# The first 1,160 steps of a fixed instruction order put into another order, in an attention and two-MoE kernel

## The chip, the cores and the metric

The kernel runs on one core of a Trainium2 chip. The metric is the device time of one execution in microseconds (us), lower is better. The engines are TensorE (in the profile PE, its weight loads PEld), VectorE (DVE), ScalarE (ACT), GpSimd (POOL) and SyncE (SP, which here issues nearly all transfers). Each engine takes its instructions strictly in the order in which the program lists them for it, and waits where an operand or a buffer isn't ready.

## The reference, cut to what matters

Inputs: q, k, v of shape (4 batches, 8 heads, 576, 64), phi of (4, 8, 576, 32), and six weight matrices in f32.

```python
a = softmax(phi, axis=2)                       # over the 576 positions
k_m = einsum('bhsm,bhsd->bhmd', a, k)          # 32 memory rows a head
v_m = einsum('bhsm,bhsd->bhmd', a, v)
attn = softmax(scale * q @ k_m.T) @ v_m        # (4, 8, 576, 64)
x = attn.transpose(0, 2, 1, 3).reshape(2304, 512)
x = (x @ w_a) * (x @ w_b) @ w_out              # 512 -> 1536 -> 512
g = x @ w_gate
out = (g / (1 + exp(-g))) * (x @ w_val) @ w2_out
```

## The kernel before, in words

The work is cut into parts, each a Python generator of a few steps; a step emits the instructions of one or two engines. A string, PLAN, lists 2,765 steps by the names of their parts, and one loop emits them in that order:

```python
    for op in PLAN.split():
        if op not in begun:
            begun[op] = work(op)
        next(begun[op], None)
```

So the seventh "p2" in PLAN is the seventh step of part p of batch 2. A dependency from each instruction to the one before it on its engine then fixes the order of all five engines.

The names, with the indices of the batch, the block of features or the tile behind them:

- P, K, L, Q, W: loads, issued by SyncE. P is phi of a batch (576 KB), K and L the first and second two pairs of heads of k and v (1,152 KB each), Q is q (1,152 KB, in two transfers), W a chunk of a weight matrix (512 KB, two words a value, to be decoded). K2, batch 2's qT, Q3 and an accumulator share one place in SBUF, called h7, one after another; phi of batches 0 and 2 and the scores of batch 0 and 2 lie in h9, of 1 and 3 in h10.
- p: the memory of a batch, 14 steps: four maxima on VectorE, one transposition (line 349), a reduction, two small products that spread the maxima (358), addition, exp on ScalarE, the sums k_m and v_m (72 products in the code, 144 matmuls in the profile, line 377, tile kv), the sums of the weights (387), reciprocals, scaling, three transpositions (412, kvT), copies to kb and vt.
- e: four additions over the weights of p. q: transpositions of q (8, 8 or 2 of them, line 437) and the copy of the result to qT, which shares the place h0, h6 or h7. s: the scores of half a batch (40 matmuls, lines 455 and 465, tile sc), maximum, subtraction, exp, denominators, product with them. o: transpositions of the normalised scores (line 502) and their split into a high and a low part, aT.
- c: decoding of a weight chunk, two steps on ScalarE (lines 235 and 237), a clamp, two VectorE operations, one or more on GpSimd. v: v_m times weights (16 matmuls, or 64 from v8 on, line 556), split into vwh and vwl.
- a and b: x @ w_a and x @ w_b of a batch and a block (12 matmuls each, line 541, s1a and s1b); b goes on with the copy, the product of the two and its split into gh and gl. d and f: their product with w_out (12 matmuls, tile s), written to the accumulators acc or added to them by VectorE (line 658).
- x: the first MoE's result is combined and split for the second. E closes the first phase: its pools are released and PSUM is given out anew. U and H are the second phase (lines 789 and 533), A and O load again the decoded weights that were parked in DRAM.

Buffers come from pools. A second table, SLOTS, gives for each kind of buffer the number of the buffer that each request in turn gets; a kind that isn't in the table gets a buffer of the pool of that kind from the builder:

```python
        n = made[key] = made.get(key, -1) + 1
        if key in slots:
            return pool.tile(shape, dt, tag=f"{tag}_{slots[key][n]}", bufs=1, name=name)
        return pool.tile(shape, dt, tag=tag, name=name)
```

In the table b2 are the four PSUM buffers of the first phase (two banks each, taken in turn by p, q, s, o, v, a, b, d and f), and raw the four buffers that weight chunks and A and O are loaded to. SyncE waits, and with it all loads listed behind, where a load's buffer isn't free. A third table, STEPS, says which engine does certain steps; it goes by the number of the part and isn't touched.

Of the kernel before, what the change touches and what calls it, by code (L numbers as in the profile page):

```python
# [18 lines left out]
def kernel(  # L19
# [874 lines left out]
    s2.1 W3.2 W12.1 b1.0 c4.1 c2.2 c9.0 p3 c9.0 s2.0 a1.0 c3.0 s2.1 q3.2 b1.1 s2.0 q3.0 v4 c3.1
    b1.0 q3.1 a1.1 q3.2 s2.0 p3 s2.1 q3.1 p3 q3.0 c3.1 c9.0 b1.0 s2.0 s3.0 c3.0 b1.1 o2.1 o2.1 o2.0
    s3.0 s3.1 o2.1 o2.0 v7 b1.1 v6 s3.0 c2.0 o2.0 a2.1 b2.1 s3.0 s3.1 W12.0 s3.1 v6 b2.0 s3.1 b1.1
    v7 s3.0 b2.1 c2.1 b1.0 v6 s3.0 s3.1 b2.0 s3.1 v7 a2.0 s3.1 W12.2 d1.0.0 W8.0 c3.0 c9.0 s3.0
    b2.0 o3.1 c2.0 o3.0 b2.1 c4.0 c2.1 d1.0.0 o3.0 c2.1 c3.0 d1.2.0 o3.1 c2.1 c2.0 c2.1 c3.2 d1.3.0
    d1.3.0 c3.2 o3.0 o3.1 b3.1 c2.0 b2.1 c4.0 c2.0 a3.1 W5.2 v8 b3.0 b3.1 a3.0 v8 c3.2 d1.2.0 c3.2
    b2.1 c12.0 c4.0 b3.1 d1.1.0 c4.0 b2.0 c3.2 c4.0 b2.0 b3.0 v8 b3.0 v8 b1.2 a1.2 c12.1 c3.2 W5.0  # L900
    c3.2 c12.0 c12.0 d2.0.0 b3.1 c12.1 d1.1.0 b1.2 v8 c12.1 c12.0 d2.1.0 d2.2.0 c12.2 c12.0 c12.0
    b3.0 c12.1 b3.1 a1.3 d2.1.0 c12.1 c12.2 d2.2.0 c12.2 d2.0.0 b0.3 b3.0 b1.2 c12.1 b1.3 d2.3.0
    b0.3 d3.2.0 b1.2 c12.2 d3.0.0 d3.2.0 b1.2 a0.3 c12.2 c12.2 b1.3 d3.1.0 c12.1 d2.3.0 c5.2 d3.3.0
    c5.0 c5.2 c8.0 d3.3.0 b1.3 c12.1 c5.0 b0.3 c5.2 c5.2 b1.3 W8.2 d3.0.0 W8.1 W13.0 c8.0 c5.0 W5.1
    d3.1.0 b0.2 c8.0 b1.3 c5.2 v9 b0.2 a0.2 v9 f0.5.2 c8.0 v9 b0.3 b0.2 c8.0 b0.2 c5.0 b0.3 b3.2 v9
# [17 lines left out]
    c15.2 c15.2 b1.6 v12 b0.6 c16.2 f1.2.4 a1.6 b2.6 c16.2 b2.7 c15.2 b3.7 b2.7 W16.1 W10.2 b0.6
    f1.3.4 c6.2 v12 b3.6 b1.6 c16.0 c9.1 b0.7 a0.7 b1.6 c16.2 b2.7 b0.7 c16.0 c16.2 c16.0 c16.1
    b0.7 c16.1 c9.2 a0.6 c6.2 f1.5.6 c9.2 f1.0.6 f1.4.6 c16.1 c16.1 f1.0.6 f1.3.6 c16.0 b0.7 c16.2
    f1.2.6 f1.1.6 b0.6 v14 b1.7 c9.2 c16.2 f1.5.6 f1.4.6 b1.6 W11.1 c16.1 c16.0 c9.2 c16.1 W17.1
    b0.6 f1.2.6 c16.0 v14 c11.1 b1.7 c16.1 f1.3.6 f1.1.6 c10.2 a1.7 v14 c16.1 b0.8 c10.2 c9.2 b0.7
    v14 b0.6 b1.7 c11.1 b1.7 b1.8 c9.2 W10.1 a1.8 b1.7 a0.8 b1.6 b0.8 c11.1 b1.8 f0.0.6 c10.1 v14
    W10.0 f0.3.6 c10.1 c11.1 f0.2.6 b0.8 c10.2 c11.1 b0.9 f0.3.6 c17.1 f0.0.6 f0.2.6 c17.1 f0.5.6
    c10.0 f0.1.6 c9.2 f0.4.6 c10.1 b1.8 c10.1 b0.9 c10.0 c10.2 c10.2 W11.0 c10.2 f0.1.6 a0.9 v15  # L930
    f0.5.6 b1.8 b1.9 W11.2 f0.4.6 a1.9 b0.8 c17.1 v15 c11.0 b0.9 c10.1 b0.8 c11.0 v15 b2.8 b1.9
    c10.2 W17.2 b1.9 v15 b3.8 v15 b2.9 a3.8 c17.1 W17.0 a2.8 b1.8 c11.0 b1.9 c10.0 b0.9 b3.8 b2.9
    a2.9 b1.9 b2.8 c11.0 c17.0 b2.9 f0.5.8 b0.9 c11.0 f0.3.8 f0.5.8 c10.0 W18.0 b3.8 f0.0.8 b2.8
    c17.0 c17.0 f0.2.8 f0.4.8 f0.1.8 c17.0 c17.1 f0.3.8 c10.0 c17.1 c17.0 c11.2 f0.0.8 v16 b3.8
    b3.9 f0.2.8 a3.9 b2.8 f0.4.8 c17.0 f0.1.8 v16 v16 c17.1 b3.9 b2.8 c11.2 v16 c11.2 b3.8 b2.9
    b0.10 b0.10 v16 A0.12 b2.9 c17.2 c17.1 a0.10 c17.2 c11.2 W18.1 A0.12 b1.11 A0.12 b3.9 c11.2
    b3.9 c11.2 W18.2 f1.0.8 b3.9 b0.11 b1.11 f1.2.8 c18.0 b0.10 c17.2 a0.11 f1.0.8 a1.11 f1.1.8
    b0.11 A0.12 f1.5.8 A0.12 f1.2.8 c17.2 f1.1.8 c18.0 f1.4.8 A0.12 c11.2 f1.5.8 c18.0 f1.3.8 b1.10
    c18.1 b0.10 b0.11 c18.1 A0.12 a1.10 b1.10 b1.11 f1.4.8 b0.11 b1.11 v17 c17.2 c18.1 b0.10 f1.3.8
    b1.10 v17 b0.11 f0.0.10 b1.11 A0.12 f0.1.10 b1.10 c18.2 v17 b1.10 f0.0.10 v17 c18.0 f0.2.10  # L940
# [185 lines left out]
```

## Time and profile before

| | |
|---|---|
| three runs | 835.71 us (median), 831.07 to 835.83 |
| the profiled execution | 836.04 us, of which 834.2 us are the span from the first to the last instruction |
| mean granted clock of TensorE | 0.985 of full speed |
| busy | TensorE 804.0 us (96%), VectorE 573.0 (69%), ScalarE 404.3 (48%), GpSimd 383.1 (46%) |
| instructions | 16,467 |
| transfers | 102.51 MB, 37.1% of the 16 DMA engines' time |

Times in the profile are us from the first instruction of the span. The change of phase (E) is at about 408 us.

### The profile page before, as it was taken

Reading aid. Unit: us, or ns where it says so; the run is one execution under the profiler, and the core shown is the slowest. Engines: PE = TensorE matmul, PEld = TensorE weight load, DVE = VectorE, ACT = ScalarE, POOL = GpSimd, SP = SyncE. Lnnn points to the kernel's source line nnn. Section 1 sums busy time; section 2 is a strip of 40 time slices with the busy share of each in tenths; the row PEclk is TensorE's granted clock in tenths of the full one; section 3 lists DMA queues with packets and bytes.
Section 4 is the critical chain, followed back from the end, with each engine's and each line's share of the span. In section 5 each row is a group of like instructions: output and inputs, shape, how many; then the busy total and the mean of one; then the engine's idle time right before and its main releaser. Section 6 shows DMA issues by size and latency. Waiting matters only on the chain.

```text
span 834.2 us, 16467 instructions
## 1 busy us (share of the span) xinstructions
PE 804.0 (96%) x6540; PEld 752.9 (90%) x6540; DVE 573.0 (69%) x1020; ACT 404.3 (48%) x790; POOL 383.1 (46%) x319
## 2 busy tenths in 40 slices
...
PEclk9789899999999999999999999999999999999999
...
GB/s 326 379 277 118 30 143 142 126 121 159 139 121 89 159 77 80 85 64 1 153 163 193 162 203 147 87 145 121 89 77 108 127 70 50 66 57 128 20 1 113
DMA packets 61772, 102.51 MB, mean 123 GB/s; under 512 B 6400, under 2 KB 35072, under 8 KB 61696
## 3 DMA queue, kind: packets, MB, share of 16 engines
q1 hardware_dynamic: 60896, 100.29, 37.1%
q8 instruction: 51, 0.84, 0.4%
q10 hardware_dynamic: 800, 1.18, 0.4%
q14 instruction: 25, 0.20, 0.1%
...
## 4 chain that ended last, share of the span: by engine, by line
PE 92%; DVE 3%; DMA 1%; ACT 1%; SPq 1%; issue 1%; DVEq 0%
PE p_a L789 18%; PE p_h L533 18%; PE s L533 15%; PE s1b L541 9%; PE p_z L789 9%; PE s1a L541 9%; PE p_c L789 4%; PE s L541 3%; PE vw L556 3%; DMA raw<-in_moe_w_b_dram 1%; PE sc L455 1%; PE kv L377 1%; PE qT L437 1%; PE sc L465 0%; SPq L325 0%
## 5 line engine op out<-in xcount | busy, mean ns | idle before, releaser
L533 PE MATMUL p_h<-o,g 128*128 128x512 f32 x648 | 163.3, 393 | 0.2 <-DVE h_2x L864 0.2
L533 PEld LDWEIGHTS p_h<-o,g 128*128 128x128 f32 x648 | 117.0, 188 | 21.3 <-DVE h_2x L864 0.5
L533 PE MATMUL s<-gh,o 128*128 128x384 f32 x480 | 125.8, 335 | 0.0
L261 POOL TENSOR_TENSOR dec_a<-dec_a,raw 128x512 int32<-128x512 int32 x48 | 66.0, 1375 | 89.1 <-DVE dec_a L249 63.2
L235 ACT ACTIVATE dec_a<-raw 128x512 f32<-128x512 f32 x72 | 48.5, 678 | 82.0 <-POOL w L259 27.1
L533 PEld LDWEIGHTS s<-gh,o 128*128 128x128 f32 x480 | 87.1, 188 | 1.1 <-issue 0.4
L864 DVE TENSOR_TENSOR h_2x<-p_h,h_2x 128x512 f32<-128x512 f32 (+1 forms) x100 | 62.0, 632 | 35.8 <-PE p_h L533 35.5
L533 PE MATMUL s<-gl,o 128*128 128x384 f32 x240 | 80.3, 334 | 0.0
L541 PE MATMUL s1b<-h_1x,vwh 128*128 128x288 f32 x384 | 69.3, 304 | 0.0
L541 PE MATMUL s1a<-h_1x,vwh 128*128 128x288 f32 x384 | 67.2, 297 | 0.3 <-DVE vwl L581 0.3
L541 PEld LDWEIGHTS s1b<-h_1x,vwh 128*128 128x128 f32 x384 | 58.4, 194 | 3.7 <-issue 1.6
L259 POOL TENSOR_TENSOR w<-dec_a,raw 128x512 int32<-128x512 int32 x24 | 31.9, 1331 | 63.8 <-DVE dec_a L249 44.3
L541 PEld LDWEIGHTS s1a<-h_1x,vwh 128*128 128x128 f32 x384 | 56.5, 189 | 2.2 <-issue 1.2
L249 DVE SCALAR_TENSOR_TENSOR dec_a<-raw,dec_a 128x512 int32<-128x512 int32 x72 | 56.0, 778 | 2.5
L174 POOL TENSOR_TENSOR w_u<-again_s,w_u 128x512 fp32r<-128x512 f32 x24 | 32.0, 1333 | 47.7 <-ACT w_u L170 47.0
L174 POOL TENSOR_TENSOR w_g<-again_a,w_g 128x512 fp32r<-128x512 f32 x24 | 31.7, 1320 | 45.7 <-ACT w_g L170 43.0
L840 ACT CAST g<-gate 128x576 fp32r<-128x576 f32 x48 | 32.1, 676 | 38.9 <-PE p_h L533 22.8
L609 DVE TENSOR_TENSOR bs<-s1a,bs 128x576 f32<-128x576 f32 x48 | 35.9, 753 | 21.9 <-PE s1a L541 19.7
L842 DVE TENSOR_TENSOR g<-gate,g 128x576 fp32r<-128x576 f32 x48 | 38.1, 799 | 17.6 <-ACT g L840 17.0
L607 ACT COPY bs<-s1b 128x576 f32<-128x576 f32 x48 | 30.4, 638 | 38.0 <-PE s1b L541 30.3
L237 ACT ACTIVATE raw<-raw 128x512 int32<-128x512 uint32 x72 | 48.4, 679 | 0.0
L807 DVE TENSOR_TENSOR p_c<-p_c,gate 128x288 f32<-128x288 f32 x48 | 22.1, 464 | 37.8 <-PE p_c L789 27.9
...
## 6 DMA issues: line engine op xcount, KB each, us to landing
...
```

The source lines that it names most:

```text
L174: nc.gpsimd.tensor_tensor(out=t[:, :, 1], in0=x, in1=f32(t[:, :, 0]), op=ALU.subtract)
L235: nc.scalar.activation(out=f32(a), in_=f32(hi), func=ACTF.Abs)
L237: nc.scalar.activation(out=lo, in_=lo.bitcast(U32), func=ACTF.Copy, scale=2.0 ** -29)
L249: nc.vector.scalar_tensor_tensor(out=a, in0=hi, scalar=-0x40000000, in1=a, op0=ALU.bitwise_and, op1=ALU.bitwise_or)
L261: nc.gpsimd.tensor_tensor(out=a, in0=a, in1=lo, op=ALU.add)
L533: nc.tensor.matmul(dst, lhsT=l, rhs=r, start=(i == 0), stop=(i == n - 1))
L541: nc.tensor.matmul(p[:, hb, 0:HB], l, x, start=(i == 0), stop=(i == n - 1))
L609: nc.vector.tensor_tensor(out=bs, in0=pa_t.pop((b, f)), in1=bs, op=ALU.mult)
L789: nc.tensor.matmul(bank(where), lhsT=x, rhs=y, start=first and t == 0, stop=t == len(terms) - 1, skip_group_check=True,)
L840: nc.scalar.copy(out=hi, in_=v)
L842: tt(out=lo, in0=v, in1=f32(hi), op=ALU.subtract)
L864: tt(out=dst, in0=src, in1=dst, op=add)
```

## The change

The first 1,160 of PLAN's 2,765 steps stand in another order: the same steps, each part's own steps in their turn. They reach from the start to the first steps of the second phase, a little behind E; the 1,605 steps after them are the same and in the same order. The table SLOTS is emptied, since it numbers requests in the old order, so the builder gives out all these buffers. The words that came with the change: the order was found by a search that counts waits for TensorE's instruction pages; nothing else.

The beginning of the diff, up to the sums of batch 2 (the seventh p2) in both orders, the stretch with the sums of batch 3 in the new order, and the end of the first phase in the new order:

```diff
     SLOTS = """
-    raw
-    0123021230120130231203210230120130230213203212130120231303210323103120120132103210321030321302310213203132321033013021031
-    pm 0101 b2
-    012301201320132031031320123012010231230123013023012301231023013012310321013021321301310213021321032312310320103230313031023132101032013021032031201231202323230132013120321031031232130312031032031312031203010230120303120132031203103201302130
...
     """.split()
...
     PLAN = """
-    P0 K0 W0.1 p0 p0 c0.1 p0 p0 L0 c0.1 W0.0 p0 p0 e0 p0 Q0 P1 c0.1 p0 c0.1 c0.0 W1.1 p0 W1.2 q0.0
-    p0 p0 p0 q0.2 c0.0 q0.0 L1 q0.2 q0.1 p1 K1 p1 c1.1 c0.0 W0.2 p1 p0 c1.1 c1.1 q0.1 c0.1 c0.0 p0
-    c1.1 p1 s0.1 p1 p1 s0.0 c1.1 s0.1 W1.0 s0.1 s0.0 c1.2 s0.1 s0.0 c0.0 v0 s0.0 s0.1 e1 Q1 c1.2 v0
-    s0.1 c0.2 c0.2 P2 p1 c1.0 L2 s0.0 W2.2 s0.0 s0.1 p1 c1.0 p1 v0 s0.0 c1.0 c1.0 p1 c1.2 K2 o0.1
-    o0.0 c1.0 P3 o0.1 q1.2 q1.0 Q2 W4.1 p1 o0.0 o0.1 p1 v1 q1.2 o0.0 p2 v1 b0.0 p1 v1 c1.2 c1.2 p2
-    c0.2 p2 b0.1 q1.0 p1 b0.0 a0.1 b0.1 c0.2 p2 c1.2 v3 c2.2 p2 a0.0 c0.2 W3.0 q1.1 b0.1 v2 c2.2
-    b0.0 c2.2 b0.1 c0.2 v3 p2 v2 c1.2 b0.0 b0.1 c0.2 s1.0 v3 p2 q1.1 p3 v2 e2 s1.1 c4.1 c4.1 s1.0
...
+    P0 L0 W0.1 W0.0 c0.1 c0.0 c0.0 p0 p0 K0 p0 c0.1 c0.1 p0 p0 p0 W1.1 c0.0 c0.1 Q0 p0 e0 P1 W1.2
+    p0 c1.1 c0.0 q0.0 p0 c1.1 p0 q0.0 q0.2 K1 p0 p0 q0.1 L1 p1 c1.1 p1 q0.2 p1 p0 p1 c1.1 p0 s0.0
+    W1.0 c0.1 c0.0 q0.1 p1 c1.2 p1 s0.1 s0.0 s0.0 v0 s0.0 s0.1 s0.1 v0 s0.0 s0.0 Q1 p1 v0 c1.1 e1
+    p1 W0.2 s0.0 s0.1 s0.1 P2 c1.0 c1.0 s0.1 s0.1 c1.0 c1.2 o0.1 L2 p1 q1.2 c1.0 p1 o0.1 p1 o0.0
+    o0.0 c0.2 q1.0 o0.1 c1.0 v1 W2.2 p1 q1.2 o0.0 c0.2 v1 p2 p1 b0.0 c1.2 p2 P3 v1 c0.2 b0.1 W4.1
+    c0.2 q1.0 a0.1 p1 b0.0 c0.2 p2 c1.2 p2 a0.0 b0.1 Q2 K2 q1.1 p2 s1.0 c2.2 c0.2 p2 c0.2 b0.0 c1.2
+    p3 q1.1 b0.0 c1.2 s1.0 s1.1 v2 L3 c2.2 b0.1 v3 v2 v3 s1.0 s1.1 q2.0 s1.0 v2 e2 v3 b0.1 s1.0
+    q2.1 s1.1 s1.1 c2.2 p2 c1.2 q2.2 c4.1 b0.0 p2 b0.1 d0.0.0 q2.1 s1.1 q2.2 c4.1 W3.1 p3 q2.0 p2
+    p2 d0.3.0 c2.2 c4.1 W3.0 p2 p3 p3 c2.2 d0.0.0 s1.0 K3 p2 p2 d0.3.0 p3 s1.1 W9.0 p2 d0.1.0 s1.0
+    c2.2 s1.1 s2.1 p3 o1.0 d0.2.0 o1.0 c4.1 c3.0 s2.1 c4.1 v5 d0.1.0 v5 c2.2 o1.1 c3.0 o1.0 s2.1 e3
+    p3 o1.1 d0.2.0 o1.1 p3 s2.0 p3 b1.0 W2.0 s2.1 s2.1 v5 p3 p3 c3.1 v4 c3.1 s2.1 c3.1 b1.1 Q3 p3
+    s2.0 a1.0 c3.0 s2.0 v4 c3.1 s2.1 b1.0 s2.0 c3.1 s2.0 q3.1 b1.1 q3.0 s2.0 s2.0 p3 v4 p3 c9.0
...
+    c11.1 W11.2 W11.0 v14 c9.2 f0.0.6 b0.9 b0.8 c9.2 f0.0.6 a0.8 c10.2 W17.2 W17.0 f0.4.6 c10.1
+    b1.8 c11.1 c11.1 c10.1 A0.12 f0.2.6 c10.2 f0.5.6 b0.8 b0.9 c10.1 f0.3.6 c10.1 f0.2.6 f0.1.6
...
+    f1.0.10 b3.11 f1.1.10 b3.10 b3.11 x1 c18.0 b3.11 x0 b3.10 x1 W19.0 b3.10 f1.3.10 f1.5.10 x1
+    f1.2.10 f1.0.10 x1 c18.1 f1.1.10 f1.4.10 f1.5.10 x1 x1 f1.3.10 f1.2.10 x1 x1 f1.4.10 E U0.12
...
```

In the old order the sums of batch 3 come after both scores of batch 2, whose part s2.0 is the last to read what Q3 overwrites, and Q3's transpositions after a1.0: on TensorE s2.1, v5, s2.0, o1.1, p3's sums, v4, b1.0, b1.1, p3's transpositions, a1.0, q3.2. In the new order it is s2.1, o1.0, d0.2.0, v5, o1.1, p3's sums, s2.0, b1.0, v4, b1.1, p3's transpositions, a1.0, q3.1.

## Rows read from the trace of the kernel before

**Rows 1.** The page: TensorE's busy time, its clock in 40 slices, instruction queue.

```profile
PE 804.0 (96%) x6540; PEld 752.9 (90%) x6540; DVE 573.0 (69%) x1020; ACT 404.3 (48%) x790; POOL 383.1 (46%) x319
...
PEclk9789899999999999999999999999999999999999
...
q8 instruction: 51, 0.84, 0.4%
```

**Rows 2.** TensorE in order of time; in brackets idle time and its end.

```profile
12.61 0.44 PE L377 MATMUL kv<-h1x,h9x 64*32 64x128 f32 x4 [0.18 <-DMA h1x<-in_v_dram]
...
23.14 0.44 PE L358 MATMUL mx<-ident,nmx 128*64 128x128 f32 x4 [0.38 <-DVE nmx L352]
25.09 1.12 PE L455 MATMUL sc<-kb,h0x 128*64 128x64 f32 x16 [1.51 <-ACT h0x L528]
...
36.34 0.88 PE L502 MATMUL aT<-ident,h9x 128*128 128x128 f32 x6 [1.01 <-DVE vwl L581]
...
410.86 1.04 PE L789 MATMUL p_z<-h_x0x,w_u 128*128 128x288 f32 x6 [2.93 <-DVE h8x L658]
```

**Rows 3.** The chain that ended last, in order of time: start, us, what.

```profile
52.33 2.17 PE kv L377 x130
54.51 2.49 issue
...
72.53 0.61 PE sc L455 x16
...
74.23 0.59 PE vw L556 x16
...
77.11 2.18 PE kv L377 x144
...
79.60 0.55 PE vw L556 x3
80.15 2.23 issue
...
91.12 1.97 PE qT L437 x18
...
113.19 1.60 PE s1b L541 x12
```

**Rows 4.** Busy time (and instructions) in stretches; then clock, DMA share, GB/s.

```profile
0.00:54.60 54.60, 36.99 (x726) 30.17 (x726) 38.52 (x80) 28.50 (x48) 18.05 (x21) 0.91 1.02 354
...
56.90:80.30 23.40, 23.16 (x378) 20.29 (x378) 17.56 (x35) 10.37 (x20) 7.71 (x7) 0.85 0.42 133
...
60.00:100.00 40.00, 37.77 (x533) 33.47 (x532) 30.75 (x60) 20.04 (x37) 11.62 (x9) 0.85 0.30 94
...
120.00:400.00 280.00, 280.00 (x2333) 271.07 (x2332) 207.25 (x297) 133.04 (x213) 137.44 (x109) 1.00 0.34 108
```

**Rows 5.** The same view of the two stretches behind the issue waits.

```profile
58.00:64.80 6.80, 6.80 (x50) 6.55 (x49) 3.29 (x6) 1.63 (x4) 1.68 (x1) 0.50 0.57 176
81.90:88.70 6.80, 6.33 (x35) 5.52 (x36) 1.97 (x6) 3.18 (x6) 1.16 (x1) 0.50 0.04 13
```

**Rows 6.** ScalarE and VectorE in order of time, where a load ended their wait.

```profile
14.00 0.69 ACT L235 ACTIVATE dec_a<-raw 128x512 f32<-128x512 f32 x1 [2.27 <-DMA raw<-in_moe_w_a_dram]
...
22.01 0.67 ACT L235 ACTIVATE dec_a<-raw 128x512 f32<-128x512 f32 x1 [2.00 <-DMA raw<-in_moe_w_b_dram]
...
20.51 0.56 DVE L336 TENSOR_TENSOR rm<-h10x 128x384 f32<-128x384 f32 x1 [1.71 <-DMA h10x<-in_phi_dram]
```

**Rows 7.** SyncE's waits from 70 to 90 us: total, times, longest.

```profile
SPq L325 <- PE sc L455: 1.9, 1, 1.9
```

**Rows 8.** Transfers issued from 76 to 86 us: KB each, us to landing.

```profile
h7x<-in_q_dram SPq DMA_DIRECT2D x1, 1024.0 KB, 8.1
```

**Rows 9.** VectorE in order of time: first and last of four waits.

```profile
59.84 0.76 DVE L477 TENSOR_REDUCE mx<-sc 128x18 f32<-128x576 f32 x1 [3.30 <-PE sc L465]
...
88.50 0.75 DVE L486 TENSOR_REDUCE den<-h9x 128x18 f32<-128x576 f32 x1 [2.94 <-ACT h9x L483]
```

More of the change, by code (lines that the diff above doesn't have):

```diff
@@ L894 @@
[L894 to L905, printed above, removed]
@@ L923 @@
[L923 to L934, printed above, removed]
@@ L935 @@
[L935 to L940, printed above, removed]
@@ new lines @@
+    d1.0.0 c2.0 c2.1 o3.0 c3.2 d1.2.0 c4.0 d1.3.0 b3.1 c4.0 b2.1 b3.1 b2.0 c3.2 c2.0 a3.1 c12.0
+    b2.1 c4.0 c3.2 b3.1 v8 b3.0 v8 a3.0 c12.1 b3.0 W5.0 v8 c12.0 c12.1 c4.0 v8 c12.0 c12.0 b1.2
+    d1.1.0 v8 b3.0 d1.1.0 b2.0 c3.2 a1.3 c12.1 b3.0 c3.2 c12.0 b0.3 a1.2 b3.1 c12.1 c12.1 b1.2 b1.3
+    b3.0 c12.2 b1.2 c12.2 c3.2 c12.2 b1.3 c12.2 d2.3.0 b0.3 b3.1 d2.1.0 c12.0 d2.2.0 c5.2 d2.3.0
+    d3.2.0 d2.1.0 c12.1 d2.0.0 c12.2 d3.0.0 b1.3 d3.1.0 b1.2 c12.2 a0.3 c12.1 d3.3.0 d2.0.0 v9
+    d2.2.0 b0.2 d3.2.0 a0.2 c5.2 d3.0.0 W8.0 c12.1 c5.2 c5.2 c5.0 c5.0 c5.0 W8.2 d3.1.0 c8.0 d3.3.0
@@ new lines @@
+    c13.2 b2.2 c14.1 c13.1 a1.4 c14.1 v10 b0.4 c4.2 c13.2 f1.5.2 a0.4 c14.1 W14.0 f1.4.2 c4.2
+    f1.3.2 c14.1 c13.2 b0.4 c14.0 b0.5 f1.1.2 c4.2 c14.1 c4.2 c4.2 f1.2.2 f1.0.2 c13.2 W6.1 c14.0
+    f1.4.2 c14.0 c14.0 b0.5 f1.3.2 c14.2 c14.2 b1.4 c14.1 c14.0 v11 c4.2 W7.1 f1.1.2 b1.5 c14.0 v11
+    c7.1 c14.1 a0.5 f1.2.2 c14.2 W7.0 a1.5 c14.2 b1.4 b0.4 f1.0.2 c7.1 v11 b0.5 b1.5 b0.4 v11 b1.5
+    b1.5 c14.1 b0.5 b3.4 c4.2 c6.1 a3.4 v11 c7.0 b3.4 c14.2 b2.5 a2.5 c7.0 b3.5 c14.2 b2.5 W6.0
+    W15.1 b1.4 b0.5 b1.5 W15.0 c7.1 c6.0 W7.2 c7.0 c7.1 b2.5 c7.0 f0.5.4 c6.1 a3.5 c6.0 b3.4 c6.0
@@ new lines @@
+    c15.1 c6.1 b3.5 c15.1 c7.1 f0.5.4 f0.1.4 c6.0 c15.0 c15.1 c7.0 c6.1 c7.2 f0.3.4 b3.5 c6.0 W9.2
+    f0.2.4 f0.0.4 c15.0 c6.1 b3.4 f0.4.4 v13 f0.3.4 f0.1.4 c7.2 v13 c15.1 f0.2.4 b2.4 c7.2 b3.4
+    f0.0.4 b2.4 b3.5 c15.0 c7.2 a2.4 b2.5 f0.4.4 v13 b3.6 c15.0 b2.6 c15.1 b2.4 v13 b3.5 v13 a3.6
+    W15.2 c15.0 c15.1 b3.7 c7.2 b2.5 f1.4.4 b2.4 b3.6 c7.2 b3.6 W6.2 a2.6 c15.0 b3.7 c15.2 b2.4
+    f1.5.4 c15.1 W9.1 c6.2 b2.6 c9.1 a3.7 c15.2 c15.1 f1.4.4 c6.2 f1.5.4 b3.7 W16.2 c9.1 W16.1
+    f1.1.4 v12 f1.3.4 c6.2 v12 c7.2 b2.6 c15.2 c15.2 f1.1.4 f1.0.4 c9.1 c6.2 f1.2.4 v12 b2.6 f1.3.4
@@ new lines @@
+    f1.0.4 c9.1 b2.7 f1.2.4 a2.7 b1.6 b3.7 b2.7 b0.6 c6.2 W16.0 v12 b2.6 c15.2 b2.7 c16.2 b3.6 a1.6
+    c6.2 c9.1 b1.6 b3.7 c16.1 c15.2 v12 b3.6 b0.7 c16.0 a0.6 b2.7 b0.6 c6.2 c16.1 c16.0 a0.7 b0.7
+    b1.6 c16.1 c16.0 f1.5.6 c16.0 b0.6 c16.1 b2.7 c16.2 f1.2.6 c9.2 c16.1 f1.0.6 f1.5.6 c16.2 W11.1
+    f1.4.6 c16.0 b0.7 f1.1.6 c16.1 c16.2 f1.3.6 c9.2 c11.1 b0.7 b1.6 f1.0.6 v14 b0.6 f1.4.6 c16.2
+    b1.7 c16.0 c16.2 c16.1 W10.2 v14 f1.2.6 b1.7 c9.2 f1.3.6 c16.1 f1.1.6 v14 c9.2 v14 W10.1 a1.7
+    b1.8 a1.8 W10.0 b1.7 b1.7 c10.2 c10.2 c11.1 b0.7 b1.8 b1.7 b1.6 b0.6 c10.2 W17.1 b0.8 c9.2
@@ new lines @@
+    c11.1 W11.2 W11.0 v14 c9.2 f0.0.6 b0.9 b0.8 c9.2 f0.0.6 a0.8 c10.2 W17.2 W17.0 f0.4.6 c10.1
+    b1.8 c11.1 c11.1 c10.1 A0.12 f0.2.6 c10.2 f0.5.6 b0.8 b0.9 c10.1 f0.3.6 c10.1 f0.2.6 f0.1.6
+    c17.1 c10.0 c10.2 v15 c10.0 f0.4.6 c10.1 f0.5.6 W18.0 a0.9 b1.9 a1.9 c17.1 b0.8 f0.3.6 c11.0
+    c10.0 c11.0 f0.1.6 c10.2 b0.8 v15 b1.9 b0.9 v15 b0.9 v15 c10.0 b2.8 b1.8 b3.8 b1.9 v15 c11.0
+    b2.9 a3.8 b1.9 b2.8 b0.9 a2.8 b1.9 b1.8 a2.9 b2.9 c17.1 b3.8 c17.1 f0.5.8 c11.0 c11.2 f0.3.8
+    c17.0 b2.9 c11.2 f0.2.8 f0.0.8 b3.8 f0.5.8 c17.0 f0.3.8 b2.8 f0.1.8 f0.2.8 c17.0 f0.4.8 c10.0
@@ new lines @@
+    c11.0 v16 c17.0 c17.1 b2.9 b2.8 f0.0.8 c11.2 c17.0 c11.2 f0.4.8 b2.9 v16 f0.1.8 A0.12 b3.9
+    c11.2 v16 b3.9 a3.9 W18.1 b3.9 b2.8 A0.12 v16 c11.2 b3.8 A0.12 b0.10 A0.12 b3.9 a0.10 b0.10 v16
+    f1.0.8 b0.11 b1.11 b3.8 a0.11 a1.11 b3.9 f1.2.8 A0.12 A0.12 b0.10 b0.11 c17.1 f1.0.8 b1.11
+    f1.5.8 c18.0 A0.12 f1.2.8 c17.2 f1.5.8 b0.11 f1.1.8 f1.3.8 f1.4.8 f1.1.8 b0.10 b1.10 b1.11
+    a1.10 b0.11 f1.3.8 f1.4.8 c18.0 b1.10 c18.1 c17.0 b0.10 v17 b1.10 b1.11 c17.2 v17 c17.1 b1.10
+    c17.1 c18.0 W18.2 c17.2 c17.2 c11.2 b0.11 A0.12 b1.11 f0.1.10 b1.10 v17 f0.1.10 c18.1 f0.0.10
@@ new lines @@
+    U0.15 U0.15 H0.13.7 U1.15 U1.15 A0.17 U1.16 O0.16 O0.17 U0.16 U1.15 U1.16 c20.2 U1.16 U1.16
+    U0.16 c21.1 H0.13.7 c21.1 U0.16 U0.15 U1.15 U1.16 c21.1 U1.16 c21.1 U0.16 U0.16 H0.15.0 U1.16
+    A0.17 U0.16 U0.16 U1.16 H0.15.0 U0.16 c21.0 O0.16 U1.16 c21.0 c20.2 U0.16 c21.1 U1.16 c21.0
+    U0.16 A0.17 U0.16 U0.16 U0.16 U1.16 W21.2 U1.16 U0.16 U1.16 c21.1 H0.15.1 c21.0 A0.17 A0.17
+    U0.16 H0.15.2 A0.17 U1.16 U1.16 U0.16 U1.17 U0.16 H0.15.1 H0.15.2 U0.17 A0.17 U1.16 U0.17 U1.16
+    A0.18 H0.15.4 c21.0 c21.2 c21.2 U1.16 A0.17 U1.16 U0.16 U1.17 c21.2 U1.17 U0.17 U1.17 H0.15.4
@@ new lines @@
+    c22.1 U0.19 H0.17.4 c23.1 U0.19 A0.19 U1.19 U0.19 A0.20 U0.19 U1.19 U1.19 U0.19 O0.19 A0.20
+    H0.17.6 H0.17.5 U1.19 H0.17.6 U1.19 U0.19 U0.19 H0.17.8 O0.20 U1.20 U0.19 c23.0 U0.20 c23.1
+    A0.20 H0.17.5 A0.20 U0.19 U0.20 c23.0 H0.17.7 U0.19 U1.20 U1.19 A0.20 U0.20 U1.19 U0.19 U1.19
+    A0.20 U1.19 U0.20 U0.20 H0.17.8 U1.20 U1.19 A0.20 A0.21 U1.20 U0.19 U0.20 A0.21 A0.22 U1.20
+    U1.20 U0.20 A0.21 U0.20 U1.20 U1.20 U1.20 U1.20 U0.20 U1.20 H0.17.7 U0.20 U1.20 U1.20 U0.20
+    U1.20 U0.20 c23.0 c23.2 c23.0 c23.1 U1.20 A0.21 H0.19.0 c23.2 U1.20 c23.2 U0.20 H0.19.0 U0.20
@@ new lines @@
+    U3.12 O1.12 U3.12 H0.23.4 U3.12 A1.13 U2.12 U2.13 H0.23.5 A1.13 U2.12 A1.13 U2.12 U3.12 U3.12
+    A1.15 U3.12 U3.12 H0.23.6 U2.13 U3.12 U3.12 A1.13 U3.12 U2.12 U3.12 U3.12 U2.13 U3.12 U3.12
+    U3.12 U2.12 U3.13 U2.13 U3.13 U3.12 U2.13 U2.13 U3.13 U3.12 U2.13 U3.12 H0.23.7 U3.13 A1.14
+    H0.23.6 U2.13 A1.16 A1.13 A1.14 U2.13 U3.13 U3.13 U2.13 U3.13 U3.13 H0.23.7 U3.13 U3.13 U2.13
+    A1.14 U2.13 x3 U3.13 U2.13 U3.13 U2.13 U3.13 U2.13 U2.13 U3.13 A1.14 A1.14 U2.13 U2.14 U3.13
+    U3.13 U3.13 U2.13 U3.14 U3.13 H0.23.8 U2.14 U3.13 U2.13 U3.14 U3.14 U2.13 U3.14 A1.14 U2.13
```

249 lines of the change are left out of this document (105 added, 144 removed).

## Prediction

> **What bounds the kernel now.** I read the page first: TensorE works 804.0 of 834.2 us, and its granted clock falls below its upper level only in the first slices and the last [rows 1]. So time is lost in two ways, idle TensorE and TensorE at its lower clock, and both lie almost wholly ahead of 110 us; from 120 to the change of phase it is never idle. TensorE's instructions in order of time, with the idle time before each in brackets, come second: 2.9 us at the change of phase, and short waits at the start, of which [rows 2] shows the ones used here. The two that matter have no releaser; they are called "issue", a wait for nothing that the profile shows. The chain that ended last shows them in place: 2.49 us inside the products of batch 2's memory (130 of 144 matmuls done) and 2.23 us three matmuls into a vw part [rows 3].
>
> Why I take these for waits for instructions: a matmul and its weight load are two instructions, so TensorE has 13,080, and the queue q8, of the kind "instruction", brought 51 packets in 0.84 MB [rows 1], so 256 instructions a packet. The two stretches of work that end at the stalls hold 1,452 and 756 [rows 4]; 756 is three times 256 less 12, and semaphore instructions, which are not counted there, can be those 12. Both stalls thus sit on a border of pages, and both come after the densest work there is: 144 small matmuls are 288 instructions, over a page, in 2.18 us [rows 3].
>
> The Trainium skill speaks against this change: "Runtime: NRT & Kernel Launch", section "Instruction fetch mechanics", has the next 16 KiB page fetched while the current one runs and calls the cost of a border mostly hidden. The trace agrees with the size of the page and differs on the cost in two of 51 places; by the rule alone the change would give the third rival's time below.
>
> After each stall the clock is at half (1.2 of 2.4 GHz) for 6.8 us, with TensorE busy nearly throughout; the page's low slices from 21 us on are a third such stretch [rows 1], behind the idle time ahead of the first scores.
>
> **The change part by part.** I sum against the profiled execution, 836.04 us (834.2 of span and 1.8 around it); the median is 0.3 below that.
>
> *The two page waits.* They took 2.49 + 2.23 = 4.7 us. Removed: -4.7.
>
> *The clock after them.* 6.8 us twice at half speed is 3.4 us of work lost each time [rows 5]. If nothing stops TensorE for long there any more: -6.8. Idle time of 1.0 us at 36.3 [rows 2] left the clock alone, so I take waits of that size as harmless and those above 2.2 us as not.
>
> *What page waits are left.* I count two instructions a matmul through the new order and start the pages where the two stalls put them (error: some 16 matmuls). The need first: 128 matmuls ahead of the first stall lie two matmuls after 52.33, and work went on at 56.99, so a page takes 4.6 us from the entry of the one before it; at the second, 128 matmuls back is about 77.4 and the end 82.37, 5.0 us. In the new order batch 2's sums come after both scores of batch 1, v2, v3, q2.0 and q2.1. The page that ends in them holds v2 and v3 (0.59 each), 16 transposes (1.97 x 16/18 = 1.75) and some 80 of the 144 matmuls (1.2): 4.1 us [rows 3] where it was 2.2. Wait: 0.5, between 0 and 0.9. The page that ends after batch 3's sums holds 78 of them (1.2), the two sums (0.3), s2.0's scores (1.7, as from 72.53 to 74.23 for another such part) and the first of b1.0 (0.4): 3.6 us. Wait: 0.7, between 0 (a fetch with the queues empty has no row; nothing else is in flight there in the new order) and 1.4. All others hold 5 us or more; from the tenth page on, 10. Together +1.2 (0 to 2.3).
>
> *The start.* K0 moves behind L0, W0.1 and W0.0, so it lands with the bytes that W0.0 ended, at 14.0 [rows 6], and batch 0's sums start 1.4 later than at 12.61 [rows 2]. P1 takes the place in bytes of W1.1 and lands at 22.0 for 20.5 [rows 6]; W1.1 comes ahead of both. This hides: the first scores waited at 25.09 for the copy of qT on ScalarE, which stood behind W1.1's first step and so behind its landing at 22.0. That step's data now lie there early, and what is late next is P1: 22.0, its four maxima, the transposition and the small products, 3.1 us after the landing as before (20.51 to 23.14 + 0.44), so 25.1. No change there. The next wait, 1.0 us of aT at 36.34, behind the last of the normalised scores, goes, since s0.0 now gets its denominators ahead of vwl and of s0.1: -1.0 (-2 to +1.4, the 1.4 if K0 comes through).
>
> *Q3.* Its place in SBUF holds batch 2's qT until s2.0's scores are done; before, SyncE waited 1.9 us for just that [rows 7], and the load then took 8.1 us [rows 8]. The old order put p3's sums behind these scores; the new one puts them ahead. Between s2.0's scores and the transposes that read Q3 TensorE now has b1.0, b1.1 and a1.0 (1.6 each, as at 113.19 [rows 3]), v4 (0.6) and p3's transposes (0.33): 5.7 us; before, the sums as well, 2.5 more. Wait: 8.1 - 5.7 = 2.4 at most. At the 354 GB/s of the first 54.6 us [rows 4] its 1,152 KB pass in 3.3, so no wait at the least. I take +1.0: the row was taken with other loads in flight, and a page wait in between is part of it.
>
> *VectorE.* It follows TensorE closely. Four of its waits come from the stalls and the slow clock, of 3.30 to 2.94 us, 9.7 in all [rows 9]; between 60 and 100 it works 30.75 us [rows 4], and without the 11.5 us of stalls and clock TensorE would be through in 28.5. So VectorE works nearly without a pause there and lags by some 2 us, which the four PSUM buffers and its 26% of idle time after 120 [rows 4] can take up. +1.0 (0 to 2.5).
>
> *The change of phase.* Before, TensorE waited 2.9 us, to 410.86, for the last additions to acc [rows 2]. Now the last addition, f1.4, stands behind four VectorE steps of x1, but two more groups of additions are done while f1.4's products run. 0 (-1 to +2).
>
> *The rest.* Chunk steps, the loads W17.2, W17.0 and A0.12, which move forward in SyncE's queue to where they block it until c10.0 and c11.0 are decoded, and the first steps of again and again_out: what stands behind these loads is work for the second phase, so nothing of the first waits for them; 0. If that cover failed, TensorE would wait for a chunk of the second phase, at its start. The emptied table of buffers costs no instruction: 0 if the builder picks the buffer that is free first.
>
> Sum: -4.7 - 6.8 + 1.2 - 1.0 + 1.0 + 1.0 = -9.3, so 826.7, or 826.5 with the median. With all terms at their good ends -14.5 (821.5), with their bad ends and the clock kept some -4 (832).
>
> **The rivals.** *One stall comes back, with its clock.* Batch 3 is the place: its page (1.4) or Q3 (2.4) stops TensorE long enough for 6.8 us at half speed, 3.4 more. For it: both are near each other and 8.1 us is the only row for Q3. Against it: Q3's row was taken with other loads in flight. In place of the +1.7 above come 2.4 + 3.4, so 830.5 to 831.
>
> *Slower: the buffers.* With the table empty every buffer of raw, of PSUM and of w is given out anew, for all 2,765 parts. The old table leaves plain rotation in 103 of the 240 takes of a PSUM buffer. If the builder's own timetable is unlike the chip's, or it rotates, a take waits for the wrong buffer, up to one group of matmuls, 1.6 us [rows 3]. From 11 such waits on (18 us) the gain above is gone and 1% more: 845. For it: nothing in the new text fixes the buffers. Against it: the old order's are not in rotation either, and TensorE has no wait between 120 and 400 [rows 4].
>
> *The stalls are not what I take them for*, or lie wherever the order puts the dense work. Then only the start is gained: 835. The count of 756 speaks against it.
>
> **How the numbers follow.** Forecast 0.62, one stall back 0.18, the buffers 0.13, no effect 0.07. One per cent, about what a measurement tells from nothing here, is 827.4 from the median; of the forecast three quarters lie below it (822 to 831 is its own range, its middle at 826.5): faster 0.46, within 0.16 + 0.18 + 0.07 = 0.41, slower 0.13. The range leaves out the buffers and the best end: 821.5 to 835.5.
>
> **What would show it.** Right: no "issue" above 1 us among TensorE's waits from 50 to 90; one stretch at half clock ahead of 110 us in place of three; batch 2's sums begun near 54 without a pause inside; a1.0 (the third group of 12 after v4) done near 79 where it was 91.1 [rows 3]; and the change of phase some 10 us earlier, with the rest as long as before (423 us). A wait of qT for DMA near 78 is the first rival; waits of TensorE for VectorE or ScalarE scattered from 120 to 400 are the buffers. I would be wrong by most if the clock fell for another cause than the stalls, or if VectorE, near its limit from 60 to 110, passed its lag on to TensorE.

## The result and the profile after

The new order takes 822.47 us in the median of 4 runs (820.82 to 822.62) beside 835.77 for the kernel before in the same session (831.07 to 835.83): ratio 0.9855, 95% interval 0.9838 to 0.9871. The profiled execution took 822.60 us, with a span of 820.8, so 13.4 us less than that of before. In the new kernel's text every line stands 13 lines higher (L377 is now L364, L541 is L528, L437 is L424).

The page, the lines that answer to [rows 1]:

```profile
PE 795.0 (97%) x6540; PEld 745.9 (91%) x6540; DVE 573.4 (70%) x1020; ACT 403.6 (49%) x790; POOL 381.7 (47%) x319
PEclk9899999999999999999999999999999999999999
q8 instruction: 51, 0.84, 0.4%
```

TensorE still fetches 51 packets of instructions, but below 9 tenths only one slice of its clock is left, the second, from 20.5 to 41 us. TensorE's instructions in order of time, idle time before each in brackets, as in [rows 2]:

```profile
14.16 0.44 PE L364 MATMUL kv<-h0x,h9x 64*32 64x128 f32 x4 [5.88 <-DMA h0x<-in_v_dram]
24.95 0.66 PE L442 MATMUL sc<-kb,h0x 128*64 128x64 f32 x16
35.61 0.63 PE L489 MATMUL aT<-ident,h9x 128*128 128x128 f32 x4 [1.47 <-DVE h9x L478]
57.83 0.52 PE L528 MATMUL s<-gh,o 128*128 128x288 f32 x2 [0.59 <-ACT h7x L515]
398.39 1.86 PE L776 MATMUL p_z<-h_x0x,w_u 128*128 128x288 f32 x12 [2.57 <-DVE h8x L645]
```

From 36 to 398 us no wait is longer than the 0.77 us before a group of qT at 37.8, and none is called "issue". The chain shows the two batches in which [rows 3] had its two waits:

```profile
54.58 2.17 PE kv L364 x140
56.77 1.02 ACT h7x L515
57.83 1.84 PE s L528 x12
68.97 2.18 PE kv L364 x144
...
72.96 6.27 DMA h7x<-in_q_dram
79.24 0.14 issue
79.37 2.16 PE qT L424 x18
```

Batch 2's sums (54.58) and batch 3's (68.97) run through without a pause. Q3's load lands at 79.24, 6.3 us after its issue, when TensorE has just come to it; it waited 0.2 us.

Two stretches give the balance: from the first product of b0.0 to the change of phase, and from 50 to 90 us. The columns are the stretch and its length, the busy time and number of instructions of PE, PEld, DVE, ACT and POOL, the granted clock, the busy share of the DMA engines and GB/s. First the kernel before:

```profile
40.76:410.86 370.10, 361.68 (x3419) 344.38 (x3420) 281.20 (x420) 178.11 (x291) 183.95 (x142) 0.98 0.37 118
50.00:90.00 40.00, 34.86 (x607) 30.52 (x600) 28.76 (x56) 19.91 (x36) 12.55 (x11) 0.83 0.41 133
```

and the kernel after:

```profile
39.90:398.39 358.49, 355.03 (x3421) 338.40 (x3419) 279.99 (x420) 176.47 (x289) 181.20 (x141) 1.00 0.37 122
50.00:90.00 40.00, 39.23 (x755) 33.71 (x752) 37.63 (x72) 25.56 (x48) 21.40 (x18) 1.00 0.54 175
25.00:33.00 8.00, 8.00 (x203) 6.88 (x205) 6.13 (x10) 3.52 (x6) 4.18 (x5) 0.57 1.07 371
```

The last line is from the one stretch at half clock that is left, behind the first scores. The long stretch is 11.6 us shorter with the same matmuls in it (3,419 and 3,421 records). TensorE's idle time in it fell by 5.0 us, of which the two page waits are 4.7, and its busy time by 6.6, the clock behind these waits. The start gives 0.9 (39.90 for 40.76) and what follows the change of phase 0.9 (422.4 for 423.3): together 13.4.

### The profile page after: what moved, and what is told of

It reads as the page before. It is cut to its first block, busy times and chain, and to the rows that moved or that the text cites. A ratio compares the mean times of both kernels' runs of the same rounds, so it can differ in the third digit from the quotient of the medians.

```text
span 820.8 us, 16480 instructions
## 1 busy us (share of the span) xinstructions
PE 795.0 (97%) x6540; PEld 745.9 (91%) x6540; DVE 573.4 (70%) x1020; ACT 403.6 (49%) x790; POOL 381.7 (47%) x319
## 3 DMA queue, kind: packets, MB, share of 16 engines
q1 hardware_dynamic: 60896, 100.29, 37.6%
## 4 chain that ended last, share of the span: by engine, by line
PE 94%; DMA 2%; DVE 2%; SPq 1%; issue 0%; ACT 0%
PE p_a L776 19%; PE p_h L520 18%; PE s L520 15%; PE p_z L776 9%; PE s1a L528 9%; PE s1b L528 9%; PE p_c L776 5%; PE s L528 3%; PE vw L543 2%; DMA h10x<-in_phi_dram 1%; PE sc L442 1%; DMA h7x<-in_q_dram 1%; PE qT L424 1%; SPq L312 1%; PE kv L364 1%; PE sc L452 0%
## 5 line engine op out<-in xcount | busy, mean ns | idle before, releaser
L528 PE MATMUL s1b<-h_1x,vwh 128*128 128x288 f32 x384 | 67.6, 298 | 0.0
L528 PE MATMUL s1a<-h_1x,vwh 128*128 128x288 f32 x384 | 67.2, 297 | 0.1
L528 PEld LDWEIGHTS s1b<-h_1x,vwh 128*128 128x128 f32 x384 | 56.5, 188 | 3.5 <-issue 3.3
L528 PEld LDWEIGHTS s1a<-h_1x,vwh 128*128 128x128 f32 x384 | 56.5, 189 | 1.4 <-issue 0.8
L236 DVE SCALAR_TENSOR_TENSOR dec_a<-raw,dec_a 128x512 int32<-128x512 int32 x72 | 53.7, 746 | 2.5
L603 ACT CAST gh<-bs 128x576 fp32r<-128x576 f32 x48 | 31.0, 673 | 34.0 <-PE s L520 29.9
```

The source lines that it names most:

```text
L236: nc.vector.scalar_tensor_tensor(out=a, in0=hi, scalar=-0x40000000, in1=a, op0=ALU.bitwise_and, op1=ALU.bitwise_or)
L528: nc.tensor.matmul(p[:, hb, 0:HB], l, x, start=(i == 0), stop=(i == n - 1))
```

## Experiments

Each ratio is to the kernel before, run on the same chip in the same session (its median there was 833.6 to 834.7 us, its runs 831.1 to 837.5).

**Only the table of buffers.**

```diff
     SLOTS = """
-    pm 0101 b2
...
     """.split()
```

> The order of before, word for word, with the table of buffers emptied, so that the builder gives out every buffer anew. Theory (the gain is the two waits for instructions, the clock after them and the start): nothing of this hangs on the buffers, so 835.8 us, within 1 us, with both waits of 2.5 and 2.2 us and three stretches at half clock still there. Rival (the gain came from the new buffers): about 822.5. Third (the new buffers cost and the new order paid for it): 838 or more.

Measured: 835.15 us, ratio 1.0005 (0.999 to 1.0019). The buffers do nothing by themselves; the rival that hung on them is out. In its profiled execution, the fastest of the ten, both waits stood at their old places, but behind the first, of 2.54 us, the clock kept its upper level:

```profile
56.92 0.42 PE L364 MATMUL kv<-h3x,h9x 64*32 64x128 f32 x8 [2.54 <-issue]
57.00:64.00 7.00, 7.00 (x89) 6.51 (x90) 4.81 (x12) 3.17 (x7) 2.86 (x4) 1.00 0.62 171
```

**More TensorE instructions ahead of the old order.** The next kernels add small matmuls to the program and move none of its parts; their result lies in unused columns of a PSUM tile and nobody reads it.

```diff
         pt = bank2("mx")
+        for _ in range(64 if b == 0 else 0):
+            nc.tensor.matmul(
+                pt[0:32, 1, 256:258], lhsT=ident[0:64, 0:32], rhs=ident[0:64, 0:2], start=True, stop=True
+            )
         nc.tensor.transpose(pt[:, 0, 0:128], m.rearrange("p j m -> p (j m)"), ident)
```

> The order and the buffers of before, with 64 more matmuls of 32x64x2 ahead of TensorE's first transposition, in time in which it waits for data, their result read by nobody. They are 128 instructions, half a page of 256, so each border falls 64 matmuls earlier in the program: both then lie in the middle of a batch's 144 sums instead of behind them, and the pages around them hold 3.3 to 3.95 us of work by the trace of before, the one in batch 1's sums 3.0. Theory: both waits of 2.5 and 2.2 us go, small ones of 0 to 1 are left, the two half-clock stretches behind them go: -10 us, 825.5 (824 to 828). Rival (the waits lie with the dense sums or with data, whatever the count): 835.8.

Measured: 833.85 us, ratio 0.9989 (0.9977 to 1.0002). The forecast failed, and for a reason that makes the run useful: the 64 calls stand in the trace as 128 matmuls and 128 weight loads, so they were not half a page but a whole one. The chain (start, length, what):

```profile
51.60 2.17 PE kv L381 x130
53.78 3.31 issue
57.08 0.45 PE kv L381 x8
...
77.11 2.18 PE kv L381 x144
...
80.14 3.14 issue
```

The two waits stand behind the same matmuls as in [rows 3] (the chain's 130 of batch 2's sums; 144 and three of the vw part), and q8 brings 52 packets in place of 51, the one more ahead of them. The chain leaves some matmuls out: in order of time 136 of batch 2's 144 are done, in both kernels.

**128 of them, and 64 ahead of the new order.** From here on a diff is against the run with 64.

```diff
-        for _ in range(64 if b == 0 else 0):
+        for _ in range(128 if b == 0 else 0):
```

> As the run before, with 128 more matmuls: 256 instructions, one whole page, so the borders lie as in before. Theory: 835.8 within 1 us, the same two waits at the same matmuls; this also shows that the matmuls themselves cost and bring nothing. Rival (the added matmuls help in another way, by work ahead of the first wait): as e2.

Measured: 839.86 us, ratio 1.0067 (1.0043 to 1.0092), with both waits at the same matmuls (4.4 and 2.2 us) and two more packets. The forecast of 835.8 missed a cost: the added matmuls ran until 15.2 us, and batch 1's kvT came 4.1 us late. That delay is most of the 4.9 us by which the span grew; the first wait is 1.9 us longer as well.

> The order of after with the same 64 matmuls. The borders move from the middle of batch 2's and 3's sums to their ends: the pages there hold 1.8 and 2.0 us of work by the trace of after (4.2 and 4.0 before the edit), and the one in batch 1's sums 2.4. Theory: waits of some 2.4 and 2.2 us return with 6.8 us at half clock behind each, and one of 1 to 2 at 34 us that lies mostly beside idle time: +11.5, so 834 (830 to 836). Rival (the new order is faster by itself, wherever the borders lie): 822.5.

Measured: 821.65 us, ratio 0.9839 (0.9813 to 0.9865), as the new kernel. The forecast of 834 rested on the same count of half a page. One whole page more moves no border, and batch 2's and 3's sums run through again. One border that cost nothing in the new kernel, in batch 1's sums, now costs a wait for instructions of 1.39 us (to 31.91). The clock kept its upper level throughout from 10 to 100 us. Only half a page remained to be tried.

**Half a page: 32 ahead of the old order.** 

```diff
-        for _ in range(64 if b == 0 else 0):
+        for _ in range(32 if b == 0 else 0):
```

> The order and buffers of before with 32 small matmuls ahead of TensorE's first transposition. The trace of the runs with 64 and 128 shows each of them as two matmuls and two weight loads, so those were one and two whole pages; 32 are 128 instructions, the half page that was meant. Each border falls 64 of the kernel's matmuls earlier: the pages that end at and behind batch 2's sums hold 3.8 and 4.0 us of work by the trace of before, the one at batch 3's 3.3, where 2.0 and 2.9 stood. From the entry of a page to the work on the next one passed 4.5 to 6.4 us at batch 2's sums in four traces and 5.0 to 6.0 at batch 3's. Theory: the waits of 2.5 and 2.2 us at the old places go, at the new ones 0 to 2 are left each, and the clock keeps its upper level behind those below 1.5: 6 to 10 us less than before, so 825 to 829. Rival (the waits lie with the dense sums or with data, whatever the count): as before, with both waits at the old matmuls.

Measured: 830.64 us, ratio 0.9954 (0.9937 to 0.9972); less gain than forecast, but the trace says where the rest went. TensorE's waits for instructions, all that there are up to 110 us, and then three stretches:

```profile
19.22 0.48 PE L441 MATMUL qT<-ident,h4x 128*128 128x128 f32 x1 [1.28 <-issue]
37.10 0.64 PE L381 MATMUL kv<-h2x,h10x 64*32 64x128 f32 x6 [3.36 <-issue]
16.00:24.00 8.00, 5.50 (x45) 4.35 (x34) 4.10 (x13) 4.87 (x10) 0.65 (x1) 0.79 1.08 370
36.00:47.00 11.00, 9.20 (x56) 7.31 (x57) 7.24 (x18) 3.27 (x8) 2.32 (x2) 0.53 1.06 383
50.00:90.00 40.00, 39.57 (x739) 34.66 (x738) 37.18 (x70) 24.92 (x45) 19.30 (x16) 1.00 0.50 157
```

From 50 to 90 us the old order now runs as the new one does: no wait, the clock at its upper level, 39.57 us of work. From batch 1's kvT to the change of phase it takes 361.3 us, where before took 371.2 and after 359.0. So 9.9 of the 12.2 us by which the new order shortens this stretch come back with the old order, by a shift of half a page alone. What eats the gain is the same thing one batch earlier: the shift puts borders behind batch 0's sums and into batch 1's, with waits of 1.28 and 3.36 us, and some 9.4 us of TensorE's work is lost to the lower clock ahead of 50 us (4.5 in before, half of the 9.0 us busy from 23.9 to 34.1).

**44 ahead of the old order.**

```diff
-        for _ in range(64 if b == 0 else 0):
+        for _ in range(44 if b == 0 else 0):
```

> As the run with 32, with 44: 176 instructions, the borders 88 matmuls earlier. The page that ends in batch 2's sums then holds 6.0 us of work, the one that ends behind them 2.4, the one at batch 3's 4.0. Theory: no wait inside batch 2's sums, one of some 1.4 behind them, 1 at batch 3's: 825 to 829, and the waits stand at other matmuls than with 32. Rival: as before.

Measured: 831.52 us, ratio 0.9967 (0.995 to 0.9985); again less gain than forecast, and for the same reason. The waits stand at other matmuls again, the larger two now in the sums of batches 0 and 1; behind batch 2's sums 0.24 us came for the 1.4 expected, at batch 3's none for 1:

```profile
19.12 0.43 PE L381 MATMUL kv<-h0x,h9x 64*32 64x128 f32 x4 [3.43 <-issue]
34.96 0.31 PE L381 MATMUL kv<-h6x,h10x 64*32 64x128 f32 x3 [1.97 <-issue]
59.72 0.34 PE L459 MATMUL sc<-kb,h6x 128*64 128x64 f32 x4 [0.24 <-issue]
```

**32 ahead of the new order.** The same edit with 32, in the kernel after.

> The order of after with the same 32. The pages that end in batch 2's and 3's sums hold 1.8 and 2.0 us of work, the one in batch 1's 2.4. Theory: waits of 2 to 4 and of 2 us come back inside or right behind the sums, with 6.8 us at half clock behind each: 11 to 13 us more than after, so 833 to 835. Rival (the new order is faster by itself, wherever the borders lie): 822.5.

Measured: 836.31 us, ratio 1.0034 (1.002 to 1.0047): 13.8 us slower than the new kernel in medians, some more than forecast, and slower than the old one, with no part moved. The waits in batch 1's and behind batch 2's sums, and the clock:

```profile
37.31 0.65 PE L368 MATMUL kv<-h2x,h10x 64*32 64x128 f32 x6 [4.44 <-issue]
64.07 0.69 PE L428 MATMUL qT<-ident,h8x 128*128 128x128 f32 x2 [3.84 <-issue]
37.00:44.00 7.00, 6.69 (x51) 5.66 (x52) 4.87 (x13) 3.74 (x8) 3.17 (x2) 0.62 0.75 265
62.00:70.00 8.00, 5.93 (x27) 5.91 (x28) 3.33 (x11) 1.47 (x4) 1.82 (x3) 0.57 0.51 177
50.00:90.00 40.00, 34.59 (x640) 29.97 (x639) 29.14 (x59) 20.18 (x36) 16.83 (x15) 0.87 0.46 149
```

Another lies in batch 3's sums (1.55 us, to 81.59), and two of 1.3 us ahead of 31 us. The stretch from 50 to 90 is that of before again. What the new order is worth, it is worth in the main through where its borders fall.

**The first 300 parts of the new order, then the old.** An entry of either list is the name of a part and how often it has come before:

```python
head = new_order[:300]
plan = head + [part for part in old_order if part not in head]
```

The table of buffers is empty in this kernel too.

> The first 300 parts in the order of after, the other 2,465 in the order in which they stand in before. Theory: what the change gains lies ahead of 100 us, so 822.5, within 1.5. Rival (the search also gained later, up to the change of phase): 825 or more.

Measured: 823.72 us, ratio 0.9881 (0.9854 to 0.9907). Its interval overlaps that of the whole change: the gain lies in the first 300 of 1,160 parts. What the other 860 bring, 1 to 2 us by the medians and the ratios, these runs can't tell from nothing.

**One part moved, two parts moved, the start alone.** All four kernels have the buffers given out anew: one has each of the two moves below, one has both, and the start alone is the sketch above with 85.

```diff
 batch 2's sums:   ... s1.0 v3 [-p2-] q1.1 p3 v2 e2 s1.1 c4.1 c4.1 s1.0 b0.0 s1.0 q2.1 s1.1 s1.0 q2.0 [+p2+] q2.1 ...
 batch 3's sums:   ... v5 [-s2.0-] o1.1 W2.0 d0.2.0 v5 o1.0 s2.1 p3 Q3 s2.1 v5 s2.1 c3.0 e3 p3 [+s2.0+] o1.1 ...
```

In the two kernels with the second move (batch 3, and both) the load Q3 stands ahead of s2.0's scores, so these read Q3's data in place of batch 2's and wait for that load. This is not the order for which the second move was forecast (Q3 behind the scores), and the wait for Q3 in these two kernels is no price of the move.

> The order of before, buffers given out anew, with one of the 2,765 parts moved: batch 2's 144 sums go behind s1.1's scores and the transpositions q2.1 and q2.0 (56 matmuls), so that the first border falls 74 matmuls into the sums instead of 130. Theory: the first wait (2.5 us) and its half clock (3.4 us) go, the second stays: -5.9, so 829.9 against 835.8. Rival (many small moves together make the gain): within 1.5 us of before.

Measured: 834.05 us, ratio 1.0004 (0.9986 to 1.0023): no gain by the median, where 5.9 was expected. The first wait for instructions is gone as forecast, but other waits stand in its place:

```profile
52.91 0.69 PE L442 MATMUL sc<-kb,h6x 128*64 128x64 f32 x16 [1.31 <-ACT h6x L515]
78.52 1.10 PE L543 MATMUL vw<-w,vt 64*32 64x256 f32 x13 [2.83 <-issue]
```

s1.1's scores now come at once behind s1.0's and wait 1.31 us for the copy of qT on ScalarE, which batch 2's sums had hidden; the second wait for instructions is 0.7 longer than in the run with the buffers alone (2.1). In the new order the same copy stands right behind batch 2's exponential and starts at 48.05, here at 51.83 behind a vw cast and a gh as well. In this execution the clock kept its upper level behind the 1.31 us:

```profile
50.00:76.00 26.00, 23.91 (x554) 20.47 (x553) 23.78 (x45) 14.73 (x27) 11.09 (x10) 1.00 0.58 191
```

The idle time hardly fell: from 50 to 90 us TensorE is idle for 5.1 us in before, 4.6 here, 6.5 in the next run, 4.6 in the one with both moves and 0.8 in the new kernel. Nor was the clock better over the ten runs: its mean is 0.987, as in the runs of before beside them.

> The order of before, buffers given out anew, with one other part moved: s2.0's scores (40 matmuls) go behind batch 3's 144 sums, so the second border falls behind 65 of the sums and then behind the scores instead of right behind the sums. Theory: the second wait (2.2 us) and its half clock (3.4 us) go, the first stays: -5.6, so 830.2. Q3 then starts after the scores as in the new order, and TensorE may wait for it by 0 to 2.4. Rival: within 1.5 us of before.

Measured: 834.88 us, ratio 1.001 (0.9992 to 1.0028): no gain, where 5.6 was expected. The second wait for instructions is gone; 1.2 us of waiting for batch 3's exponential and 1.8 for Q3 took its place. Behind these two the clock kept its level.

> Both of these moves, nothing else. Theory: -5.9 - 5.6 = -11.5, so 824.3 (823 to 827), with no wait for instructions above 1 us from 50 to 90 and the clock at its upper level there; what is left to the time of after is the start. Rival (the 1,160 new places are needed): above 829.

Measured: 832.68 us, ratio 0.999 (0.9966 to 1.0013), where 824.3 was expected. No wait for instructions is left up to 110 us, and still the clock fell twice in the profiled execution, one of the slower of the ten (837.03 of 830.09 to 838.28):

```profile
52.98 0.88 PE L442 MATMUL sc<-kb,h6x 128*64 128x64 f32 x16 [1.31 <-ACT h6x L515]
79.22 0.69 PE L442 MATMUL sc<-kb,h7x 128*64 128x64 f32 x16 [1.62 <-DMA h7x<-in_q_dram]
53.00:61.00 8.00, 8.00 (x156) 7.31 (x162) 5.32 (x10) 1.75 (x3) 5.37 (x5) 0.57 0.72 240
80.00:88.00 8.00, 8.00 (x66) 6.99 (x65) 4.10 (x12) 3.91 (x8) 1.16 (x1) 0.57 0.01 2
```

Here the clock fell behind a wait for a copy and one for a load as it did behind waits for instructions; behind the same 1.31 us for the copy in batch 2's move it did not. So my theory of the gain was too narrow: borders in the right places are needed, and a cover for every other wait near the sums as well.

> The first 85 parts in the order of after (the start, up to the first of the aT transposes), all the rest in the order of before. Theory: the start brings -1 to -2.5 us (first piece of b0.0 at 39.9 instead of 40.8, a shorter first stretch at half clock) and both waits for instructions stay, at the same matmuls: 833.3 to 834.8. Rival (the gain is in the start): below 830.

Measured: 834.61 us, ratio 1.0009 (0.9993 to 1.0025). Batch 1's kvT came 0.7 us earlier than in the run with the buffers alone, but the time shows no gain; the start is no part of the change's gain that can be measured. Both waits for instructions stayed (3.0 and 2.2 us), and again the clock kept its level behind the first:

```profile
56.87 0.42 PE L364 MATMUL kv<-h3x,h9x 64*32 64x128 f32 x8 [3.04 <-issue]
57.00:64.00 7.00, 7.00 (x90) 6.52 (x86) 4.86 (x12) 3.04 (x6) 2.45 (x3) 1.00 0.59 171
```

## Why the prediction was right, point by point

*The two page waits, -4.7.* Right, in size and in cause. That they are borders of pages, 256 instructions apart, is shown by the added matmuls: 256 or 512 instructions more leave them where they are, 128 or 176 more move them. The traces show it in a second way. Counted from the start of the program, the matmul at which a wait called "issue" of 0.2 us or more ends follows 222, 346 or 347, 475, 726, 854, 982, 1,104 or 1,106, 1,232 or 1,360 others, in whatever order the parts stand. These places lie some 126 matmuls apart, or twice that; 126 are 252 instructions, and what is missing to 256 can be instructions that the profile does not count. And each of these 24 waits ends 1.2 to 1.6 us after a packet of q8 has landed. The third rival is out. The signs named ahead came as well: one stretch at half clock, batch 2's sums from 54.6 without a pause, a1.0 done near 79, the change of phase 12.5 us earlier. One reading was off without effect: 136 of batch 2's 144 sums were done at the first wait, not 130.

The Trainium skill, "Runtime: NRT & Kernel Launch", section "Instruction fetch mechanics", calls the cost of a border mostly hidden. For 51 pages of the new kernel the trace agrees: no wait in TensorE's list of waits is called "issue". With the same instructions shifted by half a page there are five, of 1.3 to 4.4 us, and with a whole page one of 1.39; there the measurement differs.

*The clock behind them, -6.8.* The profiled executions give -6.6 of busy time between b0.0 and the change of phase. But I took the fall for certain, and it is not, so it is in part luck that this pair of executions shows nearly the full amount. Of the six traces that have the first wait (2.5 to 4.4 us), the clock fell behind it in four (before, 64, 128, batch 3's move) and stayed in two (buffers, start). The spread fits: the runs of before lie between 831.1 and 837.5, those of the new order between 820.8 and 822.6. How much of the 13.3 us in the medians is clock can be estimated from the mean granted clock that is listed for each run. One minus it, times the span, is at most what a run lost: 10.5 us in the mean of the 77 runs of before beside the experiments (clock 0.984 to 0.991), 3.5 in the four of the new kernel (0.993 to 1.000). So some 7 us are clock, the shorter stretch at the start among them, and the rest, by this estimate, is idle time.

*What page waits are left, +1.2.* Mis-sized: 0. The pages held what I had counted (4.2 us for 4.1 at batch 2, 4.0 for 3.6 at batch 3). The need was too high: I had taken 4.6 and 5.0 us from the two waits of before. In the new kernel's trace, counted two instructions a matmul, the packets of these pages landed 2.2 and 2.1 us after the entry of the page before them, where before took 3.0 and 3.6. TensorE went on 1.2 to 1.6 us after the landing wherever it had to wait in these fourteen traces, so the need was some 3.7 us (an estimate, 2.2 and 1.5). The rows "nearest" to an unknown cost were the worst cases of it.

*The start, -1.0.* It came to -0.9, but not as argued. Batch 0's sums began at 14.16. The forecast had taken 12.61 for their old start [rows 2], but eight of them stood at 11.78 in before, so they came 2.4 us later and not 1.4; it cost nothing, since the first scores stood at 24.95, on time as forecast; the wait of aT, which I said would go, grew from 1.01 to 1.47. The gain is that the half-clock stretch behind the first scores ended near 32 us where it had ended at 34, and with it 1.1 us less work was lost (3.4 for 4.5). In two later traces of the new order (64 ahead of it, and the first 300 parts) this stretch is missing altogether.

*Q3, +1.0.* Mis-sized: 0.2. The load took 6.3 us, not 8.1, beside some 6 us of TensorE's work. The bounds held it.

*VectorE, +1.0.* Mis-sized: 0. No wait of TensorE for VectorE between 38 us and the change of phase is left in the list of waits. It works 37.6 of the 40 us from 50 to 90, and no lag of it reached TensorE.

*The change of phase, 0.* 0.4 less waiting (2.57 for 2.93), and 0.9 less in all behind it; I had no term for that.

So the sum missed by 4.1 us: three terms of give-back, +3.2, of which 0.2 came, and 1.3 at and behind the change of phase; the clock and the start brought 0.2 less than their terms. The time is at the lower end of the forecast's own range (822 to 831). The bad end of that sum was added up wrongly: the bad ends of its terms give -0.9 and so 835, not -4 and 832; the range as stated (to 835.5) covers both.

*The rivals.* One stall back with its clock: not in this kernel, though half a page of shift brings it about. The buffers: out, by the run with the table alone. The order of the first 300 parts alone gives nearly all of the gain.
